# Turning the second attention's weights back unsplit, and placing them with sixteen transfers

## The chip, the cores and the metric

The kernel runs on one core of a Trainium2 chip. The metric is the device time of one execution in microseconds, lower is better. The engines are TensorE (PE in the profile, with its weight loads shown apart as PEld), VectorE (DVE), ScalarE (ACT), GpSimd (POOL) and SyncE (SP), which starts the transfers.

## The reference

Two attentions through 32 inducing points, and then a feed-forward layer with a squared ReLU, all in fp32:

```python
B, N, m, C = (4, 12480, 32, 128)          # attention
n_tokens, d_model, d_ff = (49920, 128, 2048)
...
def mab(q, kv):
    s = scale * (q @ kv.transpose(0, 2, 1))
    s = s - s.max(-1, keepdims=True)
    a = np.exp(s)
    a /= a.sum(-1, keepdims=True) + 1e-09
    return a @ kv
h = mab(I, x)          # I: the inducing points; 32 rows per batch
return mab(x, h)       # every token against those 32 rows
...
h = np.maximum(x @ w_in, 0.0)
return h * h @ w_out
```

## The kernel before

Tokens are worked on in 52 units of 960 (13 units for each of the 4 batches). A unit is two blocks of 480 tokens, and a block's 480 columns are four groups of 120. For every batch the first attention (class `First`) yields `h`, 32 rows, and `first_end` multiplies it by `w_in` once: `hw` holds `h @ w_in`, its rounded part and the rest stacked over partitions. So the second attention and the first layer of the feed-forward become one product: the attention weights of a block, 32 rows by 480 tokens, times `hw`. To get more than fp32r's precision out of fp32r products, the weights are split into a rounded part (`hi`) and the rest (`lo`), and stand stacked on 128 partitions in the tile `st` as hi, lo, hi, lo, one 480-wide slice for each of the two blocks.

How `st` comes about (class `Second`, `weigh`, from line 623): the scores of a unit (`na`, L617, written in `narrow` together with the First attention's scores of a later unit) are copied to SBUF (`ss`), turned by two fp32 transposes (`s2t`, L634) so that tokens lie on partitions, and go through maximum (L641), subtraction (L645), exponential (L648), sum (L652), a small addition on POOL (L656), reciprocal (L659) and the product `norm` (L662). The result `d` has 120 partitions and 256 columns. Then `high` (L692, a cast to fp32r into `sk`) and `low` (L696, `d` less its rounded part) split it on VectorE. `back` (L703) turns it again with four fp32r matmuls against the identity, which put block, hi or lo, and inducing point on 128 partitions (`ap`, in PSUM). `stacked` copies `ap` to `sw` in SBUF (480 columns; a helper, L247; ACT or DVE, whichever the planner finds free). `spread` (L718) starts four transfers on SP, each moving 64 partitions by 480 columns of `sw` to its place in `st`. The first unit of all (`first`) does this another way, with two tiles and without transfers.

The feed-forward part (`ffn_block`) reads `st`: 16 matmuls `h` (L821) for each block, then on ScalarE a ReLU (L833) and a square (L849), on VectorE a rounded part `hi` (L854) and the rest `lo` (L859), and on TensorE three products with the two parts of `w_out` that add up in `op` (L889). At the end of a block `op` is copied to `ot`, turned (`otp`, L909), copied to `osb` and stored.

Nothing is ordered by the loops. Each step is handed to a planner (`Plan`) as a task with an engine, an estimated duration, a due time, the tasks it needs and the PSUM banks or buffers that it takes and reads. `Plan.run` plays the tasks through: where several of an engine are ready it takes the one with the earliest due time, and the order that comes out is the fixed order in which each engine's instructions are issued. Due times repeat with a period of 32 us per unit. With t_u as the start of a unit in the plan, `narrow` for the next unit is due at t_u + 3 us, and the steps of `Second` follow at multiples of `step` = 4 us behind it: `norm` and the split at three steps, `back` at four (t_u + 19 us), `stacked` at five, `spread` at six. The next unit's first `h` is due 2 us before that unit begins (t_u + 30 us) and needs `spread`. The planner adds 2.5 us of latency to the end of a task on SP, and 0.25 us more ahead of an `h`.

Of the kernel before, what the change touches and what calls it, by code (L numbers as in the profile page):

```python
# [11 lines left out]
F32 = mybir.dt.float32  # L12
# [8 lines left out]
P = 128  # L21
# [23 lines left out]
class Plan:  # L45
# [8 lines left out]
    SWITCH = 95.0  # L54
    LATE = {"PE": 200.0, "other": 100.0}

    def __init__(self, room, begin):

        self.room, self.begin, self.tasks = room, begin, []
# [16 lines left out]
    def run(self):  # L76
# [37 lines left out]
        while len(done) < len(self.tasks):  # L114
            best = None
            for e in self.ENGINES:
                pick = None
                for t in open_[e]:
                    at = room_at(t) if t.takes else 0.0
                    if at is None:  # L120
                        continue
                    start = max(free[e], t.ready, at)
                    if e == "POOL" or (e == "DVE" and t.port):
                        start = max(start, port)
                    key = (0.0 if start <= free[e] + 40.0 else start, t.due, t.order)
                    if pick is None or key < pick[0]:
                        pick = (key, start, t)
# [27 lines left out]
def induced_attention_then_squared_relu_ffn(  # L155
# [28 lines left out]
    OB, SS, SS_NS = "DVE", "DVE", 317  # L184
    FUSED = set()
    G1_DUE, SQ_DUE, HI_DUE, LO_DUE, OP_DUE = -2000.0, 6000.0, 7000.0, 6000.0, 10500.0
# [13 lines left out]
    ps_o = ctx.enter_context(tc.tile_pool(name="ps_o", bufs=2, space=PSUM))  # L200
    ps_m = ctx.enter_context(tc.tile_pool(name="ps_m", bufs=2, space=PSUM))
    plan = Plan(dict(xn=3, early=6, xt=NU + 1, m=2, h=2, o=2, g=GB, hi=HB, lo=LB, st=2, sw=2), T_MAIN)
# [41 lines left out]
    ENG = {"ACT": nc.scalar.copy, "DVE": nc.vector.tensor_copy}  # L244
# [131 lines left out]
    class First:  # L376
        def __init__(self, b, u, due, early=False, begun=None):
# [15 lines left out]
            self.turned = []  # L393
            for k in range(2):
                self.turned.append(self.turn(k, due - lead + k * lead * 0.4, loaded))

        def turn(self, k, due, loaded):
# [18 lines left out]
            t = state["turn"] = add("PE", 440, turn, due, [loaded, state.get("turn"), self.begun] + self.turned,  # L416
# [12 lines left out]
        def weigh(self, scored, where, bank_, due):  # L429
# [25 lines left out]
            def turn_e():  # L455
                v["ep"] = bank(f"ep_{n}")
# [14 lines left out]
            t = add("PE", 300, turn_e, due + 2000, [self.powered], takes=[bank_e])  # L471
# [47 lines left out]
    def first_end(b, due, step):  # L519
# [80 lines left out]
        for k in range(F // 512):  # L600
            bw = Buffer("m" if b else "h")
            d = due + 2 * step + k * step + (WIDE_LATER if k and not b else 0)
            t = add("PE", 870, lambda k=k: wide(k), d, [s["joined"], w_ins[k]], takes=[bw])
# [4 lines left out]
    class Second:  # L608
# [13 lines left out]
        def weigh(self, scored, where, bank_, due, step):  # L622
# [8 lines left out]
            def turn():  # L631
                v["tp"] = tp = bank(f"s2t_{n}")
                for k in range(2):
# [55 lines left out]

            def high():  # L690
                v["sk"] = att.tile([TS, Q, 2, 2, M], F32R, tag="sk", name=f"sk_{n}")
                nc.vector.tensor_copy(v["sk"][:, :, :, 0, :], v["d"].rearrange("t (k q) m -> t q k m", q=Q))  # L692

            def low():
                sk = v["sk"]
                nc.vector.tensor_sub(  # L696
                    sk[:, :, :, 1, :], v["d"].rearrange("t (k q) m -> t q k m", q=Q), sk[:, :, :, 0, :]
                )

            def back():  # L700
                v["ap"] = ap = bank(f"ap_{n}")
                for q in range(Q):
                    nc.tensor.matmul(  # L703
                        ap[:, q * TS:(q + 1) * TS],
                        v["sk"][:, q].rearrange("t k a m -> t (k a m)"),
                        identr[:TS, :TS], start=(q == 0), stop=(q == Q - 1), skip_group_check=True,
                    )

            def stacked():

                v["sw"] = att.tile([P, BLK], F32R, tag="sw", name=f"sw_{n}")
                copy(ts, v["sw"], v["ap"][:, :BLK])

            def spread():
                st = att.tile([P, 2, BLK], F32R, tag="st", name=f"st_{n}")
                for k in range(2):
                    for j in range(2):
                        nc.sync.dma_start(  # L718
                            st[j * 64:(j + 1) * 64, k, :].bitcast(F32),
                            v["sw"][k * 64:(k + 1) * 64, :].bitcast(F32),  # L720
                        )
# [7 lines left out]
            t = add("PE", 150, turn, d + step, [te], takes=[bt])  # L729
            t = add("DVE", 340, top, d + step, [t], reads=[bt])  # L730
            td = add("DVE", 340, sub, d + step, [t], reads=[bt])
# [4 lines left out]
            tp = add("DVE", 340, norm, d + 3 * step, [t])  # L736
# [5 lines left out]
            else:  # L742
                th = add("DVE", 210, high, d + 3 * step, [tp], port=True)
                tl = add("DVE", 335, low, d + 3 * step, [th], port=True)
            if first:
                t1, last = [], None
                for k in range(2):
                    ba = Buffer("m")
                    t = add("PE", 460, lambda k=k: back1(k), d + (4 + k) * step, [ts_[k]], takes=[ba])
# [5 lines left out]
            t = add("PE", 460, back, d + 4 * step, [tl], takes=[ba])  # L755
            ts = add(ST, (455, 565), stacked, d + 5 * step, [t], takes=[bw], reads=[ba])
            self.ready = [add("SP", 1000, spread, d + 6 * step, [ts], takes=[self.bst], reads=[bw])] * 2

    def narrow(second, f, g, due, step, begun=None, early=False):
# [28 lines left out]
        if f:  # L788
            f.weigh(t, lambda: v["a"][:, 2 * TS:4 * TS], bank_a, due)
        if second:  # L790
            second.weigh(t, lambda: v["a"][:, :2 * TS], bank_a, due, step)
# [8 lines left out]
    def ffn_block(b, u, k, second, t0, g_open, by_pairs, fused):  # L800
# [7 lines left out]
        def quad(j, last):  # L808
# [4 lines left out]
            for i in range(2):  # L813
# [27 lines left out]
                if fused(j):  # L841
                    relus.append(add("DVE", 1090, relu, d + 1000, [t] + g_open + relus, late=100, **kw))
# [8 lines left out]
            def high(h):  # L851
                if h.start == 0:
                    v["hi"] = place(f"{n}_{j}", "hi")
                ENG["ACT" if fused(j) else "DVE"](v["hi"][:, h], v["g"][:, h])  # L854

            def low(h):
                if h.start == 0:
                    v["lo"] = place(f"{n}_{j}", "lo")
                nc.vector.tensor_sub(v["lo"][:, h], v["g"][:, h], v["hi"][:, h])  # L859

            from_hi, from_lo = [], []
            for x, h in enumerate(halves):
# [4 lines left out]
                if fused(j):  # L867
                    th = add("ACT", 1706, lambda h=h: high(h), due + 5700, need, late=0, **kw)
                else:
                    sq = add("ACT", 166 + 1540 * part_of, lambda h=h: square(h), due + SQ_DUE + off, need, reads=[bg], late=0)  # L870
                    th = add("DVE", 70 + 1000 * part_of, lambda h=h: high(h), due + HI_DUE + off, [sq] + from_hi, port=True,
                             late=0 if x or len(halves) > 1 else LATE_HI, **kw)
                tl = add("DVE", 70 + 2000 * part_of, lambda h=h: low(h), due + LO_DUE + off + 900 * (len(halves) > 1), [th] + from_lo, port=True, late=100.0 * fused(j),
                         takes=[blo] if x == 0 else [], reads=[bg, bhi] + ([blo] if x else []))
# [7 lines left out]
            for x, (m, i) in enumerate(order):  # L882
# [12 lines left out]
                last = add("PE", 438, products, due + OP_DUE - ahead + 600 * x, [from_[i if len(halves) > 1 else 0], last, w_outs[j]],  # L895
# [118 lines left out]
```

## Time and profile before

| | us |
|---|---|
| three runs | 1733.75, 1734.13, 1734.22 (median 1734.13) |
| the profiled execution, its own time | 1733.3 |
| its span, first to last instruction | 1731.5 |
| TensorE busy | 1709.3 |
| VectorE busy | 1649.1 |
| ScalarE busy | 1625.9 |

The profile shows one execution. A busy time is the union of an engine's instructions. Rows of groups give a source line, the engine, the operation, `out<-in` tiles, sizes and a count; behind the first bar stand the busy microseconds and the mean nanoseconds of one instruction; behind the second the idle time of the engine just before them and what ended it. Rows in order of time begin with the start and the duration in microseconds. Rows by window begin with the window and its length, and give the busy time of each engine (or of the chosen tile's instructions) with counts, the granted clock, the share of the DMA engines that is busy and GB/s. Matmuls are pipelined: one of 480 columns is shown with some 0.38 us, but the next starts about 0.2 us after it. The granted TensorE clock over the span was 0.998 of full speed.

### The profile page before, as it was taken

The page shows a single profiled execution, that of the slowest core. Times are in us where ns is not written, and L with a number is a line of the kernel's source. Part 1 is how long each engine was busy: PE and PEld are TensorE (multiplying, and loading weights), DVE is VectorE, ACT ScalarE, POOL GpSimd, SP SyncE. Part 2 cuts the span into 40 slices and gives each one's busy share as a digit, 9 for nine tenths or more (in the row PEclk, how much of TensorE's full clock was granted, in tenths as well). Part 3 has the DMA queues.
Part 4 walks back from the last instruction along what each step waited for, and adds up shares of the span by engine and source line. Part 5 has one row for each costly group of instructions (what it writes and reads, how often), then busy time and mean ns, then how long its engine had stood idle before and what let it go on. Part 6 is the DMA issues. An engine that isn't in the chain of part 4 may idle for free.

```text
span 1731.5 us, 24820 instructions
## 1 busy us (share of the span) xinstructions
PE 1709.3 (99%) x9629; PEld 1426.2 (82%) x9629; DVE 1649.1 (95%) x1744; ACT 1625.9 (94%) x1725; POOL 24.0 (1%) x57
## 2 busy tenths in 40 slices
PE   7899999999999999999999999999999999999998
PEld 5588888888888888888878888888888888888887
DVE  5999999999999999999999999999999999999998
ACT  6799999999999999999999999999999999999997
POOL 0000000000000000000000000000000000000000
PEclk9999999999999999999999999999999999999999
DMA  9211211211121111212211111111110111111110
GB/s 243 50 48 48 51 41 49 52 45 48 28 53 46 46 47 46 58 37 50 52 35 47 46 46 47 50 43 47 41 28 23 45 25 35 35 35 35 27 43 23
DMA packets 34068, 82.00 MB, mean 47 GB/s; under 512 B 4983, under 2 KB 21079, under 8 KB 33951
## 3 DMA queue, kind: packets, MB, share of 16 engines
q1 hardware_dynamic: 33951, 80.42, 18.7%
q8 instruction: 76, 1.25, 0.3%
q14 instruction: 41, 0.34, 0.1%
HBM read 29.77 MB, written 25.56 MB: 32 GB/s over the span
## 4 chain that ended last, share of the span: by engine, by line
PE 96%; DVE 1%; DMA 1%; ACT 1%; issue 0%; SPq 0%; DVEq 0%; ACTq 0%
PE op L889 63%; PE h L821 21%; PE otp L909 3%; PE xtp L409 2%; PE na L617 2%; DMA xn<-in_x_dram 1%; PE ap L703 1%; PE nb L479 1%; PE na L424 1%; PE wp L575 1%; PE s2t L634 1%; PE ep L458 1%; DVE lo L859 0%; PE sp L424 0%; ACT e L450 0%
## 5 line engine op out<-in xcount | busy, mean ns | idle before, releaser
L859 DVE TENSOR_TENSOR lo<-g,hi 128x1920 fp32r<-128x1920 f32 (+1 forms) x419 | 896.6, 2140 | 19.5 <-DVE hi L854 0.9
L833 ACT ACTIVATE g<-h 128x960 f32<-128x960 f32 x832 | 794.3, 979 | 26.3 <-PE h L821 23.6
L849 ACT ACTIVATE g<-g 128x1920 f32<-128x1920 f32 (+1 forms) x419 | 757.3, 1808 | 3.9
L821 PE MATMUL h<-st,hw 128*128 128x480 f32 x1664 | 512.2, 387 | 2.1 <-ACT g L833 1.2
L854 DVE CAST hi<-g 128x1920 fp32r<-128x1920 f32 (+1 forms) x419 | 480.2, 1146 | 32.2 <-ACT g L849 20.5
L889 PE MATMUL op<-hi,wo_lo 128*128 128x480 f32 x1664 | 500.5, 383 | 0.0
L889 PE MATMUL op<-hi,wo_hi 128*128 128x480 f32 x1664 | 467.9, 389 | 0.1
L889 PE MATMUL op<-lo,wo_hi 128*128 128x480 f32 x1664 | 435.4, 382 | 0.0
L889 PEld LDWEIGHTS op<-lo,wo_hi 128*128 128x128 f32 x1664 | 309.8, 188 | 50.4 <-DVE lo L859 0.2
L889 PEld LDWEIGHTS op<-hi,wo_lo 128*128 128x128 f32 x1664 | 309.4, 188 | 48.7 <-issue 1.0
L889 PEld LDWEIGHTS op<-hi,wo_hi 128*128 128x128 f32 x1664 | 301.7, 188 | 55.2 <-issue 12.6
L821 PEld LDWEIGHTS h<-st,hw 128*128 128x128 f32 x1664 | 302.1, 188 | 47.7 <-ACT g L833 2.7
L247 DVE COPY osb<-otp 120x512 f32<-120x512 f32 x104 | 71.0, 683 | 2.6 <-PE otp L909 2.5
L409 PE MATMUL xtp<-ident,xn 120*128 120x120 f32 x416 | 61.5, 275 | 4.5 <-DMA xn<-in_x_dram 4.2
L409 PEld LDWEIGHTS xtp<-ident,xn 120*128 120x128 f32 x416 | 50.7, 145 | 17.4 <-issue 4.0
L247 ACT COPY ot<-op 128x480 f32<-128x480 f32 x80 | 45.4, 567 | 20.4 <-PE op L889 20.3
L909 PE MATMUL otp<-ident,ot 128*120 128x128 f32 x416 | 62.5, 273 | 1.0 <-ACT ot L247 0.6
L909 PEld LDWEIGHTS otp<-ident,ot 128*120 128x120 f32 x416 | 50.6, 137 | 15.1 <-DVE hw L584 1.8
L247 ACT COPY xt<-xtp 128x480 f32<-128x480 f32 x66 | 37.6, 574 | 13.4 <-PE xtp L409 13.4
L656 POOL TENSOR_SCALAR z<-z 120x8 f32<-120x8 f32 x51 | 23.3, 456 | 1649.0 <-DVE z L652 1649.0
L703 PEld LDWEIGHTS ap<-identr,sk 120*128 120x128 f32 x204 | 30.0, 190 | 3.7
L479 PE MATMUL nb<-xn,et 120*32 120x128 f32 x752 | 32.8, 277 | 0.0
(113 smaller groups left out, 690.4 us busy)
## 6 DMA issues: line engine op xcount, KB each, us to landing
xn<-in_x_dram SPq DMA_DIRECT2D x52, 480.0 KB, 4.3
st<-sw SPq DMA_DIRECT2D x204, 120.0 KB, 2.3
out_dram<-osb SPq DMA_DIRECT2D x51, 480.0 KB, 3.3
hi_i<-in_moe_w_in_dram SPq DMA_DIRECT2D x2, 512.0 KB, 13.3
lo_i<-in_moe_w_in_dram SPq DMA_DIRECT2D x2, 512.0 KB, 15.4
hi_o<-in_moe_w_out_dram SPq DMA_DIRECT2D x2, 512.0 KB, 11.5
lo_o<-in_moe_w_out_dram SPq DMA_DIRECT2D x2, 512.0 KB, 11.2
out_dram<-osb SPq DMA_DIRECT2D x2, 240.0 KB, 2.6
```

Source lines behind the costliest of these rows:

```text
L247: ENG[task.by](dst, src)
L409: nc.tensor.transpose(v["tp"][:, t * TS:(t + 1) * TS], self.xn[:, 4 * k + t, :], ident[:TS, :TS])
L479: nc.tensor.matmul(where[q * M:(q + 1) * M, :], self.et[:, k, q * M:(q + 1) * M], self.xn[:, 2 * q + k, :], start=(k == 0), stop=(k == 1),)
L617: nc.tensor.matmul(where[q * M:(q + 1) * M, :], self.s["hT"][:, :M], self.s["xt"][self.u][:, q * 2 * TS:(q + 1) * 2 * TS], start=True, sto ...
L703: nc.tensor.matmul(ap[:, q * TS:(q + 1) * TS], v["sk"][:, q].rearrange("t k a m -> t (k a m)"), identr[:TS, :TS], start=(q == 0), stop=(q ...
L821: nc.tensor.matmul(c["hp"][:, l, :BLK], s["hw"][:, f * P:(f + 1) * P], s["st", u][:, k, :], start=True, stop=True,)
L833: nc.scalar.activation(g, h, AF.Relu)
L849: nc.scalar.activation(v["g"][:, h], v["g"][:, h], AF.Square)
L854: ENG["ACT" if fused(j) else "DVE"](v["hi"][:, h], v["g"][:, h])
L859: nc.vector.tensor_sub(v["lo"][:, h], v["g"][:, h], v["hi"][:, h])
L889: nc.tensor.matmul(w["op"][:, :BLK], wo[:, 4 * j + l, :], v[name][:, l, :], start=(j == x == 0 and l == 0), stop=(j == NQ - 1 and x == 5 a ...
L909: nc.tensor.transpose(tp[:TS, q * P:(q + 1) * P], w["ot"][:, q * TS:(q + 1) * TS], ident)
```

## The change

For every unit but the first of all, `norm`'s result is turned back as it is, by two fp32 transposes, one per block. On 128 partitions lie now column group and inducing point, in the columns the two blocks of 120 tokens. The split follows in PSUM's layout: `high` copies 240 columns to fp32r (ACT or DVE), `low` on DVE subtracts that from what PSUM holds. Both parts go to `sw`. Since a column group's 32 rows must now go to other columns, and hi and lo are each wanted twice, `spread` starts sixteen transfers, each moving 32 partitions by two runs of 120 columns (30 KB).

The planner's table of costs is altered with it: `spread` is charged 1600 ns instead of 1000, PE tasks carry a mode, changes of mode and some durations have new values. The diff brings several new switches as well (turning pairs together, work on POOL, another division of PSUM banks, a preference for the same mode), all at the value at which the old way is kept: `PAIR = XTP_PAIR = False`, `STICK = 0.0`, `FUSED`, `POOL_HI` and `POOL_LO` empty, `MB = 2`.

```diff
-            def high():
-                v["sk"] = att.tile([TS, Q, 2, 2, M], F32R, tag="sk", name=f"sk_{n}")
-                nc.vector.tensor_copy(v["sk"][:, :, :, 0, :], v["d"].rearrange("t (k q) m -> t q k m", q=Q))
-
-            def low():
-                sk = v["sk"]
-                nc.vector.tensor_sub(
-                    sk[:, :, :, 1, :], v["d"].rearrange("t (k q) m -> t q k m", q=Q), sk[:, :, :, 0, :]
-                )
-
             def back():
                 v["ap"] = ap = bank(f"ap_{n}")
-                for q in range(Q):
-                    nc.tensor.matmul(
-                        ap[:, q * TS:(q + 1) * TS],
-                        v["sk"][:, q].rearrange("t k a m -> t (k a m)"),
-                        identr[:TS, :TS], start=(q == 0), stop=(q == Q - 1), skip_group_check=True,
+                for k in range(2):
+                    nc.tensor.transpose(
+                        ap[:, k * TS:(k + 1) * TS],
+                        v["d"][:, k * Q:(k + 1) * Q].rearrange("t q m -> t (q m)"), ident[:TS, :TS],
                     )
 
-            def stacked():
-
-                v["sw"] = att.tile([P, BLK], F32R, tag="sw", name=f"sw_{n}")
-                copy(ts, v["sw"], v["ap"][:, :BLK])
+            def high():
+                v["sw"] = att.tile([P, 2, 2 * TS], F32R, tag="sw", name=f"sw_{n}")
+                copy(th, v["sw"][:, 0], v["ap"][:, :2 * TS])
+
+            def low():
+                nc.vector.tensor_sub(v["sw"][:, 1], v["ap"][:, :2 * TS], v["sw"][:, 0])
 
             def spread():
                 st = att.tile([P, 2, BLK], F32R, tag="st", name=f"st_{n}")
-                for k in range(2):
-                    for j in range(2):
+                for q in range(Q):
+                    for a in range(4):
                         nc.sync.dma_start(
-                            st[j * 64:(j + 1) * 64, k, :].bitcast(F32),
-                            v["sw"][k * 64:(k + 1) * 64, :].bitcast(F32),
+                            st[a * M:(a + 1) * M, :, q * TS:(q + 1) * TS].bitcast(F32),
+                            v["sw"][q * M:(q + 1) * M, a % 2, :].rearrange("p (k t) -> p k t", k=2).bitcast(F32),
                         )
...
-            tp = add("DVE", 340, norm, d + 3 * step, [t])
+            tp = add("DVE", 340, norm, d + 3 * step, [t], port=True)
...
-                th = add("DVE", 210, high, d + 3 * step, [tp], port=True)
-                tl = add("DVE", 335, low, d + 3 * step, [th], port=True)
...
-            t = add("PE", 460, back, d + 4 * step, [tl], takes=[ba])
-            ts = add(ST, (455, 565), stacked, d + 5 * step, [t], takes=[bw], reads=[ba])
-            self.ready = [add("SP", 1000, spread, d + 6 * step, [ts], takes=[self.bst], reads=[bw])] * 2
+            t = add("PE", 219, back, d + 4 * step, [tp], takes=[ba], mode="t")
+            th = add(ST, (255, 317), high, d + 5 * step, [t], takes=[bw], reads=[ba])
+            tl = add("DVE", 317, low, d + 5 * step, [th], reads=[ba, bw])
+            self.ready = [add("SP", 1600, spread, d + 6 * step, [tl], takes=[self.bst], reads=[bw])] * 2
...
-    SWITCH = 95.0
+    SWITCH = {"t": 0.0, "r": 0.0, "n": 100.0, None: 0.0}
...
+        return cls.SWITCH[old] if new is None else 92.0 if new == "n" != old else 0.0
...
-                if t.mode != mode:
-                    start += self.SWITCH
+                start += self.switch(mode, t.mode)
...
-            t = add("PE", 300, turn_e, due + 2000, [self.powered], takes=[bank_e])
+                t = add("PE", 219, turn_e, due + 2000, [self.powered], takes=[bank_e], mode="t")
...
-            t = add("PE", 150, turn, d + step, [te], takes=[bt])
+                t = add("PE", 219, turn, d + step, [te], takes=[bt], mode="t")
...
-        t = add("PE", 510 * bool(second) + 520 * bool(f) + 450 * bool(g), go, due, needs, mode="n",
+        t = add("PE", 445 * bool(second) + 410 * bool(f) + 470 * bool(g), go, due, needs, mode="n",
```

More of the change, by code (lines that the diff above doesn't have):

```diff
@@ L185, in induced_attention_then_squared_relu_ffn @@
     FUSED = set()
+    POOL_HI = set()
+    POOL_LO = set()
+    FUSED_DUE = 3000.0
+    STICK = 0.0
+    PAIR, PAIR_DUE, XTP_PAIR = False, 3000.0, False
+    MB = 2
     G1_DUE, SQ_DUE, HI_DUE, LO_DUE, OP_DUE = -2000.0, 6000.0, 7000.0, 6000.0, 10500.0
@@ L243, in induced_attention_then_squared_relu_ffn @@
     add = plan.add
-    ENG = {"ACT": nc.scalar.copy, "DVE": nc.vector.tensor_copy}
+    ENG = {
+        "ACT": nc.scalar.copy, "DVE": nc.vector.tensor_copy,
+        "POOL": lambda dst, src: nc.gpsimd.tensor_scalar(dst, src, 1.0, 0.0, ALU.mult, ALU.add),
+    }
     def copy(task, dst, src):
@@ L393, in __init__, with turn_both, turn, turned @@
             self.turned = []
+            if XTP_PAIR and not early:
+                self.turn_both(due - lead, loaded)
+                return
             for k in range(2):
                 self.turned.append(self.turn(k, due - lead + k * lead * 0.4, loaded))
+        def turn_both(self, due, loaded):
+            banks = [Buffer("m"), Buffer("m")]
+            tp = {}
+            def turn():
+                self.xt = self.s["xt"][self.u] = xt_pool.tile([C, UNIT], F32, tag="xt", name=f"xt_{self.n}")
+                for k in range(2):
+                    tp[k] = bank(f"xtp_{self.n}_{k}")
+                    for t in range(4):
+                        nc.tensor.transpose(tp[k][:, t * TS:(t + 1) * TS], self.xn[:, 4 * k + t, :], ident[:TS, :TS])
+            t = state["turn"] = add("PE", 750, turn, due, [loaded, state.get("turn"), self.begun], mode="t",
+                                    takes=banks + [self.bt], reads=[self.bx])
+            for k in range(2):
+                def turned(k=k):
+                    copy(self.turned[k], self.xt[:, k * BLK:(k + 1) * BLK], tp[k][:, :BLK])
+                self.turned.append(add(XT[k], (440, 567), turned, due + XT_DUE, [t], reads=[banks[k], self.bt]))
         def turn(self, k, due, loaded):
@@ L620, in score, with weigh @@
                 )
-        def weigh(self, scored, where, bank_, due, step):
+        def weigh(self, scored, where, bank_, due, step, pair=None):
             v = {}
@@ L728, in weigh, with turn_both, with_e @@
             te = add(SS, SS_NS, evict, d, [scored], reads=[bank_])
-            t = add("PE", 150, turn, d + step, [te], takes=[bt])
-            t = add("DVE", 340, top, d + step, [t], reads=[bt])
-            td = add("DVE", 340, sub, d + step, [t], reads=[bt])
+            if pair is None:
+                t = add("PE", 219, turn, d + step, [te], takes=[bt], mode="t")
+            else:
+                def turn_both():
+                    turn()
+                    pair["e"]()
+                def with_e(turn_e, powered):
+                    pair["e"] = turn_e
+                    pair["task"] = add("PE", 438, turn_both, d + PAIR_DUE, [te, powered], takes=[bt], mode="t")
+                    return pair["task"]
+                pair.update(bank=bt, turn=with_e)
+                t = pair["first"]()
+            t = add("DVE", 340, top, d + max(step, PAIR_DUE if pair else 0), [t], reads=[bt])
+            td = add("DVE", 340, sub, d + max(step, PAIR_DUE if pair else 0), [t], reads=[bt])
             tp = add("ACT", 307, power, d + 2 * step, [td])
@@ L894, in quad @@
                 begin = j == x == 0
-                last = add("PE", 438, products, due + OP_DUE - ahead + 600 * x, [from_[i if len(halves) > 1 else 0], last, w_outs[j]],
+                last = add("PE", 438, products, due + OP_DUE - ahead + 600 * x, [from_[min(i, len(from_) - 1)], last, w_outs[j]],
                            takes=[bo] if begin else [], reads=[buf] + ([] if begin else [bo]))
```

91 lines of the change are left out of this document (58 added, 33 removed).

## The prediction

> **What bounds the kernel now.** I read the page first: its busy shares, then its chain of work that ended last.
>
> ```profile
> span 1731.5 us, 24820 instructions
> PE 1709.3 (99%) x9629; PEld 1426.2 (82%) x9629; DVE 1649.1 (95%) x1744; ACT 1625.9 (94%) x1725; POOL 24.0 (1%) x57
> PE 96%; DVE 1%; DMA 1%; ACT 1%; issue 0%; SPq 0%; DVEq 0%; ACTq 0%
> ```
>
> TensorE (PE) is busy in all but 22 us of the span, and the chain of waits runs through it for 96%. VectorE (DVE) and ScalarE (ACT) are nearly as full, but nothing waits for them for long. So the end is set by the amount of work on PE, and by any moment at which PE stands still. A microsecond taken from DVE or ACT is worth nothing by itself; one PE idle per unit is worth 51 us.
>
> Next I asked the view by tile for `st`, the stacked weights, and counted the `h` matmuls, their readers, with the view by windows.
>
> ```profile
> L821 PE MATMUL h<-st,hw x1664: 372/381/778, 62.8 to 1716.0; 128*128 128x480 f32 x185
> L718 SPq DMA_DIRECT2D st<-sw x204: 461/590/1428, 86.1 to 1683.9; - x102
> DMA to landing us min/median/max: 2.1/2.3/4.1
> ```
> ```profile
> 0.00:610.44 610.44, 168.22 (x545) 0.99 0.24 61
> 610.44:642.60 32.16, 9.71 (x32) 1.00 0.19 47
> ```
>
> 52 units share 1664 `h` matmuls, 32 each, so matmul 545, at 610.44, is the first of unit 17 (counted from 0): the first that reads the weights which unit 17's transfers bring. Unit 18's first comes 32.2 us later. Now the whole making of those weights, from the view of instructions in order of time (single instructions picked out by narrow windows):
>
> ```profile
> 598.83 0.42 DVE L662 TENSOR_TENSOR d<-d,z 120x256 f32<-120x256 f32 x1
> 600.23 0.29 DVE L692 CAST sk<-d 120x256 fp32r<-120x256 f32 x1
> 602.50 0.42 DVE L696 TENSOR_TENSOR sk<-d,sk 120x256 fp32r<-120x256 f32 x1
> 603.29 0.56 PE L703 MATMUL ap<-identr,sk 120*128 120x120 f32 x4
> 604.56 0.53 ACT L247 CAST sw<-ap 128x480 fp32r<-128x480 f32 x1
> 605.12 0.47 SPq L718 DMA_DIRECT2D st<-sw  x1
> 605.64 0.59 SPq L718 DMA_DIRECT2D st<-sw  x1
> 606.28 0.59 SPq L718 DMA_DIRECT2D st<-sw  x1
> 606.91 0.59 SPq L718 DMA_DIRECT2D st<-sw  x1
> 610.22 0.38 PE L889 MATMUL op<-lo,wo_hi 128*128 128x480 f32 x1
> 610.44 0.38 PE L821 MATMUL h<-st,hw 128*128 128x480 f32 x1
> ```
>
> The normalised weights are ready at 599.25, the turn back starts at 603.29, the copy ends at 605.09, and the four transfers start 0.52, 0.64 and 0.63 us after one another. The last lands about 2.3 us after its issue, at 609.2, and `h` reads at 610.44 behind PE work without a gap: 1.2 us to spare. The transfers are hidden now, but by little.
>
> **PE's own work.** Four `back` matmuls become two fp32 transposes, which are what `s2t` does now. From the view of groups, 300 to 1600 us:
>
> ```profile
> L703 PE MATMUL ap<-identr,sk 120*128 120x120 f32 x164 | 22.8, 261 | 0.0
> L634 PE MATMUL s2t<-ident,ss 128*120 128x128 f32 x80 | 15.2, 272 | 0.0
> ```
>
> Four `ap` take 22.8/41 = 0.56 us, two transposes 15.2/40 = 0.38, so a unit saves 0.18 and 51 units 9 us; counted by halves (two of four matmuls, 0.28 a unit) it is 14. I take 10.
>
> **DVE and ACT.** The split moves behind the turn: the cast and subtraction on DVE (0.29 + 0.42) and a 480-wide copy (0.53 on ACT) become a 240-wide copy and a subtraction that reads PSUM. Their nearest rows:
>
> ```profile
> L645 DVE TENSOR_TENSOR d<-s2t,mx 120x256 f32<-120x256 f32 x40 | 16.8, 420 | 0.4
> L247 ACT COPY et<-ep 120x256 f32<-120x256 f32 x30 | 11.0, 367 | 0.3 <-PE ep L458 0.2
> ```
>
> DVE saves about 0.3 us a unit and ACT 0.16. PE's work covers both engines, so I count nothing; without that cover it would be some 15 us of DVE. The split's bank stays taken for one DVE instruction longer; PE has other work then, nothing counted.
>
> **The planner.** Every new switch (PAIR, XTP_PAIR, STICK, FUSED, the POOL sets, MB = 2) stands at its neutral value. New durations, modes and the port on `norm` can only reorder. The most a better order can give is the 22 us that PE idles; what a worse one costs no row shows. Zero, with 10 us either way.
>
> **The transfers: when `back` runs and when `h` wants its weights.** The planner lets the earliest due go first when PE has a choice: `back` is due 19 us after a unit's start, the next unit's first `h` 30 us after it. Neither due changes. Today `back` comes late because it waits for cast and subtraction; after the change it needs only `norm`, so it can run 0.37 after it (the step from 602.92 to 603.29): 599.6, which is 10.8 us ahead of 610.44 and about its due. In unit 18 `norm` is further ahead, and the due takes over:
>
> ```profile
> 628.34 0.42 DVE L662 TENSOR_TENSOR d<-d,z 120x256 f32<-120x256 f32 x1
> 633.46 0.56 PE L703 MATMUL ap<-identr,sk 120*128 120x120 f32 x4
> 642.63 0.38 PE L821 MATMUL h<-st,hw 128*128 128x480 f32 x1
> ```
>
> 13.9 us from `norm` to `h`, but 11 between the two dues. I take 10.8 for all 51 units. The planner charges the sixteen transfers 1.6 us plus 2.5 to land, so it sees its weights ready in good time and has no reason to move `h` back.
>
> The way from `back` to the landing: two transposes 0.38; the wait for the copying engine 0.71 (603.85 to 604.56); copy 0.37; the wait for DVE, between nothing and one `lo` (2.15) and 1.98 for `sk` at 600.52, taken as 1.5; subtraction 0.42; to SP 0.03. That makes 3.4.
>
> Then sixteen transfers of 32 rows with two runs each, 64 pieces like the 64 rows of today. No row has that shape. The nearest is today's `st<-sw`, 0.52 for the first and 0.635 for each later one; from below, loads issued one right after another at the start, and one alone:
>
> ```profile
> 2.07 0.41 SPq L390 DMA_DIRECT2D xn<-in_x_dram  x1
> 2.53 0.40 SPq L335 DMA_DIRECT2D hi_i<-in_moe_w_in_dram  x1
> 2.97 0.51 SPq L390 DMA_DIRECT2D xn<-in_x_dram  x1
> 616.89 0.33 SPq L390 DMA_DIRECT2D xn<-in_x_dram  x1
> ```
>
> They stand 0.45 apart. I take `st`'s own price, the same rows between the same memories: the sixteenth starts 0.52 + 14 x 0.635 = 9.4 us after the first and lands at 9.4 + 2.3 = 11.7. At 0.45 it would be 15 x 0.45 + 2.1 = 8.9. Each transfer carries both blocks' columns, so the first `h` needs all sixteen. They land 3.4 + 11.7 = 15.1 us after `back`, and PE arrives after 10.8: it stands still 4.3 us a unit, 51 x 4.3 = 219 us (1.5 us, 77 in all, at 0.45). Behind the waiting `h` on PE stand the older block's `op` products and the next `xtp`, ready but not reachable, and ACT and DVE run dry behind PE. On SP the sixteen end some 10 us after about 603, before the load at 616.89; the next store is later still. Both keep their time.
>
> **What standing still does to the clock.** The windows with their granted clock (the number after the busy shares), and PE's gaps before them:
>
> ```profile
> 48.00:50.00 2.00, 0.38 (x3) 0.32 (x3) 2.00 (x8) 1.06 (x2) 0.00 (x0) 0.59 0.84 209
> 50.00:52.00 2.00, 1.62 (x11) 0.56 (x11) 1.65 (x5) 0.00 (x0) 0.00 (x0) 0.50 0.17 61
> 52.00:54.00 2.00, 2.00 (x7) 0.85 (x4) 1.17 (x3) 0.00 (x0) 0.00 (x0) 0.50 0.00 0
> 54.00:56.00 2.00, 2.00 (x9) 1.14 (x7) 1.43 (x4) 0.79 (x2) 0.00 (x0) 0.71 0.00 0
> 60.00:64.00 4.00, 2.26 (x18) 1.46 (x16) 3.91 (x10) 1.88 (x6) 0.00 (x0) 1.00 0.00 0
> ```
> ```profile
> 45.73 0.43 PE L458 MATMUL ep<-ident,e 128*120 128x128 f32 x2 [1.20 <-ACT e L450]
> 49.89 0.77 PE L562 MATMUL htp<-join,hacc 128*128 128x128 f32 x2 [1.62 <-DVE join L558]
> ```
>
> With gaps no longer than 1.62 us the clock was halved for about 1.6 + 2 + 2 + 1.2 = 6.8 us; at 60 to 64 us, with PE idle for 1.7 of 4, it held. A gap of 4.3 us is longer than any of these. If half of such a stretch, 3.4 us, falls on matmuls, a stall costs another 1.7; I take it for four stalls in five, 1.4 a unit, 70 us. The ends are 0 and 3.4 a unit. By the Trainium skill ("TensorE: Matmul & The Clock Gate", Part 1) the clock halves only after a whole idle window of about 3.4 us, in a row of windows that runs freely; a 4.3 us gap covers one about one time in four, and by that rule I estimate 20 us here and a sum near 1960. The trace above differs, as it halved with shorter gaps.
>
> **The sum.** The profiled execution took 1733.3 us (span 1731.5 and 1.8 around it), 0.05% under the 1734.13 median. 1733.3 - 10 + 219 + 70 = 2012 us, slower.
>
> **The rivals.** *All hidden.* If the transfers start no more than 0.35 us apart, the last lands 3.4 + 15 x 0.35 + 2.1 = 10.8 after `back`, just in time; only PE's saving is left: 1723. For it speaks the lone load's 0.33; against it, the median `st` transfer keeps SP for 0.59 by itself. The Trainium skill ("DMA: Bandwidth & Descriptors", Issuing engines are not separate DMA queues) would have it so: the time a sequencer needs to start a transfer is usually small beside the transfer. Here it is 0.635 against 2.3, and sixteen make 10; the trace disagrees. Chance 0.12.
>
> *Half hidden.* The transfers stand 0.45 apart, like loads: 1.5 us a unit, too short to halve the clock: 1733 - 10 + 77 = 1800. For it speaks the halved row count, against it the equal number of pieces. Chance 0.14.
>
> *Stall without the clock.* As forecast, but the clock holds, as at 60 to 64 us: 1733 - 10 + 219 = 1942. Chance 0.2.
>
> *Stall with more.* The whole 6.8 us of each halved stretch fall on matmuls: 1723 + 51 x (4.3 + 3.4) = 2116, or over 2130 if a transfer costs more than 0.635 by its two runs a row. Over 2130: 0.04.
>
> **How the numbers follow.** The forecast has 0.5. From 1780, under the half-hidden case, to 2130, over the full price of the clock, the range holds all but the hidden case and the top, and a little of the half-hidden one. A measurement of this kernel can tell about 0.2%, 3.5 us, from no change. Faster 0.12 (hidden), same 0.02 (hidden but for the last 0.2 us a unit), slower 0.86.
>
> **What would show it.** In the changed profile: 816 `st<-sw` transfers in groups of sixteen, about 10 us long; a gap of about 4 us before the first `h` of each unit, put down to a DMA; PE's share near 85%; granted clock under 0.95; `back` starting within 1 us of `norm` or about 11 us of PE work before `h`. Starts 0.35 us apart or less would make it wrong, and so would `h` standing 15 us of PE work behind `back`.

## The result, and the profile after

The changed kernel takes 2075.74 us (median of 4 runs, 2075.06 to 2077.81) against 1734.18 (median of 4 runs beside it) before: ratio 1.197, 95% interval 1.195 to 1.198. Its profiled execution took 2075.06, 341.8 more than the 1733.3 of the one before.

The page of the changed kernel, span, busy shares and the chain of work that ended last:

```profile
span 2073.2 us, 25260 instructions
PE 1806.5 (87%) x9527; PEld 1489.5 (72%) x9527; DVE 1635.7 (79%) x1707; ACT 1627.7 (79%) x1711; POOL 31.6 (2%) x57
PE 50%; SPq 21%; DVE 15%; issue 6%; DMA 5%; ACT 3%; POOL 0%; DVEq 0%; ACTq 0%
```

PE is busy for 87% instead of 99%, and the chain, 96% on PE before, now runs for a fifth through SP's own instructions. Two things stand in the first two lines: PE idles 2073.2 - 1806.5 = 267 us where it idled 22, and its busy time has grown although two of its matmuls per unit were taken away. The views by tile and of waits say for what PE idles:

```profile
L753 SPq DMA_DIRECT2D st<-sw x816: 585/594/1921, 81.3 to 2026.1; - x164
DMA to landing us min/median/max: 1.8/1.9/3.7
```
```profile
PE h L878 <- DMA st<-sw: 217.6, 45, 6.6
```

The idle time before `h`, in the kernel before and in the changed one:

```profile
L821 PE MATMUL h<-st,hw 128*128 128x480 f32 x1664 | 512.2, 387 | 2.1 <-ACT g L833 1.2
L878 PE MATMUL h<-st,hw 128*128 128x480 f32 x1664 | 543.5, 410 | 244.2 <-DMA st<-sw 217.6
```

Each of the 816 transfers keeps SP for 0.59 us, like the 204 before, though it has half the rows and a quarter of the bytes (before and after it moves 64 contiguous pieces). Unit 17 in order of time, from the turn back to the unit's first `h` (line 878; matmul 545 of its kind, as before; the row with sixteen transfers gives their whole stretch):

```profile
709.14 0.37 PE L737 MATMUL ap<-ident,d 120*128 120x120 f32 x2
709.55 0.41 DVE L264 CAST sw<-ap 128x240 fp32r<-128x240 f32 x1
709.87 2.15 DVE L916 TENSOR_TENSOR lo<-g,hi 128x1920 fp32r<-128x1920 f32 x1
709.99 13.11 SPq L753 DMA_DIRECT2D st<-sw  x16
711.94 1.16 DVE L911 CAST hi<-g 128x1920 fp32r<-128x1920 f32 x1
713.01 0.40 DVE L747 TENSOR_TENSOR sw<-ap,sw 128x240 fp32r<-128x240 f32 x1
724.55 0.67 PE L878 MATMUL h<-st,hw 128*128 128x480 f32 x2 [4.13 <-DMA st<-sw]
```

The first transfer, of a rounded part, starts before the subtraction has run; the second carries a rest and waits for it, and with it all behind it on SP. From 713.44 fifteen follow, the last starts at 722.50 and lands 1.9 later, at 724.4. PE has been idle for 4.13 us. These rows were picked out with narrow windows:

```profile
713.44 0.59 SPq L753 DMA_DIRECT2D st<-sw  x1
722.50 0.59 SPq L753 DMA_DIRECT2D st<-sw  x1
```

The windows around that gap, with the granted clock behind the busy times:

```profile
720.00:724.00 4.00, 0.42 (x5) 0.19 (x2) 3.15 (x3) 0.58 (x2) 0.00 (x0) 1.00 0.22 51
724.00:726.00 2.00, 1.45 (x5) 1.26 (x6) 0.00 (x0) 0.75 (x1) 0.00 (x0) 0.83 0.00 0
726.00:728.00 2.00, 2.00 (x6) 1.65 (x5) 0.00 (x0) 1.92 (x2) 0.00 (x0) 0.50 0.00 0
728.00:730.00 2.00, 2.00 (x9) 1.71 (x8) 0.94 (x1) 0.97 (x1) 0.00 (x0) 0.81 0.00 0
```

Just when PE has work again, its clock is halved for 0.7 + 2 + 0.8 = 3.4 us. The mean granted clock over the span is 0.933, which makes (1 - 0.933) x 2073.2 / 0.5 = 278 us at half speed.

### The profile page after: what moved, and what is told of

The parts are those of the page before. It is cut to its first block, busy times and chain, and to the rows that moved or that the text cites. A ratio compares the mean times of both kernels' runs of the same rounds, so it can differ in the third digit from the quotient of the medians.

```text
span 2073.2 us, 25260 instructions
## 1 busy us (share of the span) xinstructions
PE 1806.5 (87%) x9527; PEld 1489.5 (72%) x9527; DVE 1635.7 (79%) x1707; ACT 1627.7 (79%) x1711; POOL 31.6 (2%) x57
## 4 chain that ended last, share of the span: by engine, by line
PE 50%; SPq 21%; DVE 15%; issue 6%; DMA 5%; ACT 3%; POOL 0%; DVEq 0%; ACTq 0%
PE op L955 31%; SPq L753 21%; PE h L878 12%; DVE lo L916 6%; DVE hi L911 5%; DMA st<-sw 5%; PE na L659 1%; PE nb L521 1%; ACT g L906 1%; ACT g L890 1%; DVE sw L264 1%; PE otp L975 1%; DVE sw L747 1%; PE na L463 1%; PE xtp L448 1%
## 5 line engine op out<-in xcount | busy, mean ns | idle before, releaser
L890 ACT ACTIVATE g<-h 128x960 f32<-128x960 f32 x832 | 786.3, 976 | 358.1 <-PE h L878 355.3
L878 PE MATMUL h<-st,hw 128*128 128x480 f32 x1664 | 543.5, 410 | 244.2 <-DMA st<-sw 217.6
L878 PEld LDWEIGHTS h<-st,hw 128*128 128x128 f32 x1664 | 320.2, 201 | 307.2 <-issue 258.5
L955 PE MATMUL op<-hi,wo_lo 128*128 128x480 f32 x1664 | 528.3, 401 | 0.0
L955 PE MATMUL op<-hi,wo_hi 128*128 128x480 f32 x1664 | 506.0, 414 | 0.0
L955 PEld LDWEIGHTS op<-hi,wo_lo 128*128 128x128 f32 x1664 | 330.2, 201 | 54.8 <-issue 1.4
L955 PEld LDWEIGHTS op<-hi,wo_hi 128*128 128x128 f32 x1664 | 323.7, 203 | 58.6 <-issue 12.0
L955 PEld LDWEIGHTS op<-lo,wo_hi 128*128 128x128 f32 x1664 | 319.9, 193 | 54.9 <-DVE lo L916 0.3
L264 ACT COPY xt<-xtp 128x480 f32<-128x480 f32 x97 | 53.4, 554 | 45.9 <-PE xtp L448 45.9
L659 PE MATMUL na<-xt,hT 128*32 128x240 f32 x416 | 32.7, 386 | 0.4 <-DVE hT L264 0.4
## 6 DMA issues: line engine op xcount, KB each, us to landing
hi_i<-in_moe_w_in_dram SPq DMA_DIRECT2D x2, 512.0 KB, 13.1
```

The lines of the kernel that those rows point to most:

```text
L264: ENG[task.by](dst, src)
L659: nc.tensor.matmul(where[q * M:(q + 1) * M, :], self.s["hT"][:, :M], self.s["xt"][self.u][:, q * 2 * TS:(q + 1) * 2 * TS], start=True, sto ...
L878: nc.tensor.matmul(c["hp"][:, l, :BLK], s["hw"][:, f * P:(f + 1) * P], s["st", u][:, k, :], start=True, stop=True,)
L890: nc.scalar.activation(g, h, AF.Relu)
L955: nc.tensor.matmul(w["op"][:, :BLK], wo[:, 4 * j + l, :], v[name][:, l, :], start=(j == x == 0 and l == 0), stop=(j == NQ - 1 and x == 5 a ...
```

## The experiments

The theory is that of the prediction: sixteen transfers start one after another on SP, PE reaches the next unit's first `h` before the last has landed, stands still, and then works at a halved clock. The rivals: the split behind the turn comes too late whatever the number of transfers; small pieces are slow to land; the planner's new order costs by itself. `e1` to `e12` count the runs.

### Four transfers instead of sixteen (e1)

```diff
-                for q in range(Q):
-                    for a in range(4):
+                for k in range(2):
+                    for j in range(2):
                         nc.sync.dma_start(
-                            st[a * M:(a + 1) * M, :, q * TS:(q + 1) * TS].bitcast(F32),
-                            v["sw"][q * M:(q + 1) * M, a % 2, :].rearrange("p (k t) -> p k t", k=2).bitcast(F32),
+                            st[j * 64:(j + 1) * 64, k, :].bitcast(F32),
+                            v["sw"][k * 64:(k + 1) * 64].rearrange("p a t -> p (a t)").bitcast(F32),
```

> The changed kernel, but its weights leave in four transfers of 64 partitions by 480 columns instead of sixteen; the same bytes land in st, in other columns than they should (the pieces are not put in their right places). Theory, the count of transfers on SP: the last lands some 4.2 us after the subtraction, 4.3 + 4.2 = 8.5 us after the turn back, where PE arrives after 10.7; no gap before a unit's first h, clock at 0.998, 1715 to 1730 us, about 10 below the kernel before. Rival, the split behind the turn comes too late: the chain from the turn to the subtraction is unchanged, so gaps of some us per unit remain and the time stays over 1800. Rival, the planner's new order costs: no gap before h, but a time above 1745.

1724.8 us, ratio 0.994 (0.993 to 0.995). The page:

```profile
span 1723.7 us, 24412 instructions
PE 1701.4 (99%) x9527; PEld 1416.5 (82%) x9527; DVE 1633.2 (95%) x1707; ACT 1616.4 (94%) x1711; POOL 31.6 (2%) x57
```

The readers of `st`:

```profile
L878 PE MATMUL h<-st,hw 128*128 128x480 f32 x1664 | 509.8, 388 | 0.4 <-ACT g L890 0.4
```

With everything of the change but the count of transfers (and the pieces' right places in `st`), the loss is gone, PE no longer waits before `h`, and its saving is there: 10 us against the kernel before in the medians, 7.8 between the profiled spans. The split behind the turn and the new order cost nothing that can be seen. This run is also the measure for the rest: against it the changed kernel's PE idles 266.7 - 22.3 = 244 us more and is busy for 1806.5 - 1701.4 = 105 us more with the same 9527 matmuls. 244 + 105 is the whole distance between the two spans, 349.5.

### Sixteen transfers in the kernel before (e2)

```diff
-                for k in range(2):
-                    for j in range(2):
-                        nc.sync.dma_start(
-                            st[j * 64:(j + 1) * 64, k, :].bitcast(F32),
-                            v["sw"][k * 64:(k + 1) * 64, :].bitcast(F32),
-                        )
+                for q in range(Q):
+                    for j in range(2):
+                        for k in range(2):
+                            nc.sync.dma_start(
+                                st[j * 64:(j + 1) * 64, k, q * TS:(q + 1) * TS].bitcast(F32),
+                                v["sw"][k * 64:(k + 1) * 64, q * TS:(q + 1) * TS].bitcast(F32),
+                            )
```

> The kernel before, its four transfers cut into sixteen (64 partitions by 120 columns each, the same bytes in the right places). Theory, the count alone: 0.52 + 13 x 0.635 us until the fifteenth starts and 1.9 to land make 10.7 us from the copy, where the first h came 6.0 us after it on average: PE stands 4.7 us per unit, 240 us, and the halved clock adds about 110: 2030 to 2110 us. Rival, the split in PSUM or the planner's order causes the loss: the kernel keeps within 1% of 1734. Rival, half the rows make a transfer dear: starts here, with 64 rows each, are clearly less than 0.6 us apart and the time is under 1900.

2091.8 us, ratio 1.206 (1.204 to 1.208). Nothing but the number of transfers differs from the kernel before. The readers of `st`, and the transfers:

```profile
L822 PE MATMUL h<-st,hw 128*128 128x480 f32 x1664 | 550.1, 412 | 245.1 <-DMA st<-sw 233.0 <-issue 10.7 <-ACT st L247 0.6
L719 SPq DMA_DIRECT2D st<-sw x816: 461/595/1714, 87.2 to 2041.3; - x164
```

Before `h` PE idles 245.1 us, 4.8 a unit, as in the changed kernel. With 64 rows a transfer keeps SP as long (0.595) as with 32, so the rows set no price here; each is 64 pieces in both. Count alone is enough, and e1 and e2 together clear the other parts of the change.

### The gap filled with idle work (e3)

```diff
                         c["hp"] = ps_h.tile([P, 2, 512], F32, tag="h", name=f"h_{n}_{2 * j + i}")
+                        if k == j == i == 0 and (b, u) != units[0]:
+                            for _ in range(20):
+                                nc.tensor.matmul(
+                                    c["hp"][:, 0, :BLK], s["hw"][:, :P], s["hw"][:, :BLK], start=True, stop=True,
+                                )
```

> The changed kernel, with 20 matmuls of 480 columns put ahead of each unit's first h, into the same PSUM bank that it then overwrites; they need nothing that is late and fill about 4.1 us of the gap of 4.2 to 6.6. Theory, the halved clock costs over 100 us of the 341: the gap shrinks to under 1.5 us, the clock goes back to above 0.98, and the time falls to 1950 to 1980 although PE has 51 x 4.1 us more to do. Rival, the halved clock costs nothing of its own (other engines set the pace then): the time stays at 2075 within 10. A third way, that the gap is not a wait for transfers at all: the matmuls add their 210 us and the time goes to 2280.

1989.1 us (ratio 1.146, 1.145 to 1.148), 87 less than the changed kernel and just above the range expected. Page and readers of `st`:

```profile
span 1986.7 us, 27300 instructions
PE 1933.5 (97%) x10547; PEld 1606.6 (81%) x10547; DVE 1635.0 (82%) x1707; ACT 1621.7 (82%) x1711; POOL 31.6 (2%) x57
L883 PE MATMUL h<-st,hw 128*128 128x480 f32 x1664 | 512.1, 389 | 30.5 <-DMA st<-sw 23.2 <-issue 5.9 <-ACT g L895 1.3
```

The kernel does 1020 useless matmuls more and is faster. The mean clock is 0.995; the real `h` take 389 ns in the mean, as without stalls, and 30.5 us of gaps are left. The halved clock is thus a cost of its own, and the gap is a real wait: filling it added nothing. It came out above the range in part because the 20 matmuls made PE busy for (1933.5 - 1701.4) / 51 = 4.6 us a unit and not 4.1, longer than half of the gaps of the changed kernel; the rest stays open.

### Another order of the same transfers (e4)

```diff
-                for q in range(Q):
-                    for a in range(4):
+                for a in (0, 2, 1, 3):
+                    for q in range(Q):
```

> The changed kernel with its sixteen transfers in another order: the eight that carry the rounded parts first, then the eight that carry the rest. Now the second transfer waits for the subtraction, 3.4 us after the first starts. Theory, SP's time counts from when its transfers can run without a wait: the last starts 9.4 us after the first instead of 12.4, the gap falls from 4.8 to about 1.8 us, the clock recovers in part: 1820 to 1925 us. Rival, the landing of many small pieces is the limit and not their start: the last lands as late as now and the time stays above 2030.

1890.5 us, ratio 1.089 (1.088 to 1.091). The readers, and one group of sixteen on SP:

```profile
L878 PE MATMUL h<-st,hw 128*128 128x480 f32 x1664 | 523.5, 397 | 114.8 <-DMA st<-sw 89.4 <-issue 12.2 <-ACT xt L264 12.0
654.05 10.23 SPq L753 DMA_DIRECT2D st<-sw  x16
```

The same transfers end in 10.2 us instead of 13.1, since eight of them run while the subtraction is still waiting for VectorE. The gaps fall to 114.8 us, 2.3 a unit. One line of order in a queue is worth 185 us. Landing was not the limit.

### The planner told the true cost (e5)

```diff
-            self.ready = [add("SP", 1600, spread, d + 6 * step, [tl], takes=[self.bst], reads=[bw])] * 2
+            self.ready = [add("SP", 10500, spread, d + 6 * step, [tl], takes=[self.bst], reads=[bw])] * 2
```

> The changed kernel, with the planner told what sixteen transfers cost on SP (10500 ns instead of 1600), nothing else. Theory, a loop from one unit's first h to the next: first h, narrow, some 13 us to norm, then 15.2 us to the landing, over 32 us in all; moving h back in the order brings no other work into the gap. The planner's own plan grows by 200 us, and the time stays far above the kernel before: 1880 to 2060 us, the gap spread over other places. Rival, the 1600 in the table is the fault and an honest cost lets PE's other work cover the wait: 1720 to 1760 us.

1909.6 us, ratio 1.100 (1.098 to 1.102). No gap is left before a unit's first `h`, as the planner now puts other work there, but the time is not given back. Its readers and the longest wait of PE's weight loads:

```profile
L878 PE MATMUL h<-st,hw 128*128 128x480 f32 x1664 | 514.5, 397 | 46.5 <-ACT g L890 46.5
PEld h L878 <- ACT g L890: 80.4, 106, 2.3
```

PE now waits for ScalarE's ReLU instead, for 46.5 of its 113.5 us of idle time. It is also busy for 1795.8 - 1701.4 = 94 us more than in e1, of which its clock (0.987) accounts for no more than (1 - 0.987) x 1909.3 = 25; the rest stays open. So the 1600 was wrong, but an honest number alone does not hide the transfers. The loop that the expectation names fits the time; that it is the loop and nothing else was not shown.

### The chain moved ahead (e6, e8)

```diff
-    PERIOD, START, T_MAIN, NARROW, STEP = 32000.0, 2600.0, 46000.0, 3000.0, 4000.0
+    PERIOD, START, T_MAIN, NARROW, STEP = 32000.0, 2600.0, 46000.0, 1000.0, 3000.0
...
-            self.ready = [add("SP", 1600, spread, d + 6 * step, [tl], takes=[self.bst], reads=[bw])] * 2
+            self.ready = [add("SP", 7000, spread, d + 6 * step, [tl], takes=[self.bst], reads=[bw])] * 2
```

e8 is this edit alone; e6 has e4's order too.

> The rounded parts' transfers first, as before, and the whole chain moved ahead: narrow due 1 us after a unit's start instead of 3, steps of 3 us instead of 4, SP charged 7000. In the plan the turn back now stands 12.9 to 15.1 us ahead of the next unit's first h instead of about 11, and the last landing is due 12.4 after the turn. Theory: gaps under 0.5 us, clock above 0.99, PE's saving is all that is left: 1720 to 1740 us. Rival, earlier dues take places from PE's other work, which then waits for VectorE and ScalarE: no gap before h, but 1745 to 1800 us.

> The changed kernel with the chain moved ahead (narrow at 1 us, steps of 3 us, SP charged 7000) and the transfers in the change's own order. The last landing comes 15.2 us after the turn, and the plan puts 12.9 to 15.1 between turn and h. Theory: a gap of 0.2 to 1 us in most units and 2 in some, clock near 0.99: 1735 to 1790 us; the lead alone gives back more than the order alone (1890). Rival, what the order alone gave came from the wait of SP's queue and not from the lead: still above 1850.

e6: 1734.4 us, ratio 0.9995 (0.9986 to 1.0003). e8: 1747.4, ratio 1.007 (1.006 to 1.009). The readers of `st` in e6:

```profile
L878 PE MATMUL h<-st,hw 128*128 128x480 f32 x1664 | 509.5, 387 | 6.0 <-ACT g L890 4.5 <-DMA st<-sw 1.2 <-issue 0.3
```

Sixteen transfers can be hidden: their waits shrink to 1.2 us. But 10 us against e1 are lost elsewhere, some 6 of them as PE's idle time (1731.8 - 1703.1 = 28.7 against 22.3), and PE's saving is spent. The lead alone is worth far more than the order alone (1747 against 1890).

### Half of the transfers on POOL (e7, e11)

```diff
-            self.ready = [add("SP", 1600, spread, d + 6 * step, [tl], takes=[self.bst], reads=[bw])] * 2
+            ts = add("SP", 1600, spread, d + 6 * step, [th], takes=[self.bst], reads=[bw])
+            tq = add("POOL", 1600, lambda: spread(nc.gpsimd, (1, 3)), d + 6 * step, [tl, ts], reads=[bw, self.bst])
+            self.ready = [tq] * 2
```

`spread` takes a queue and the two places that it fills. e11 adds narrow at 2.5 us, steps of 3.5 us and a charge of 100 on POOL.

> The changed kernel; the eight transfers of the rounded parts start on SP as soon as those are copied, the eight of the rest start on POOL after the subtraction. No transfer of POOL's is in any trace here, so its price is open. Theory, what is serial is the issuing engine: SP's eight end 5.1 us after the copy; if POOL starts its eight as fast as SP, the last lands 4.3 + 5.1 + 1.9 = 11.3 us after the turn against 10.7 available: 1740 to 1800 us; at 1 us each on POOL 14.2 us and 1930 to 1990. Rival, the transfers are serial in the DMA engines that both share: the last lands about 14 to 15 us after the turn whatever the queue, with POOL's instructions short, and the time stays above 1950.

> Eight transfers on SP and eight on POOL, with narrow due at 2.5 us and steps of 3.5 us; the plan puts the turn 12.9 us ahead of the first h in most units. The last landing came 10.9 us after the turn with this split. Theory: no gap in most units, 1725 to 1745 us. Rival, POOL's transfers hold up its small addition in the chain to norm and VectorE beside it: no gap before h, but 1760 to 1815.

e7: 1817.4 us, ratio 1.048 (1.046 to 1.049); e11: 1745.3, ratio 1.006 (1.004 to 1.007). In e7:

```profile
L755 SPq DMA_DIRECT2D st<-sw x408: 585/594/1730, 84.1 to 1766.1; - x136
L755 POOL DMA_DIRECT2D st<-sw x408: 533/536/1538, 87.8 to 1767.7; - x136
```

POOL starts a transfer in 0.53 us, SP in 0.59 beside it: what is serial is the engine that starts them, not what moves the bytes. It shows best in unit 14 of e11, where both start at nearly the same time and each takes for its eight about what SP takes alone, 5.1 us:

```profile
514.62 5.07 SPq L755 DMA_DIRECT2D st<-sw  x8
515.36 5.21 POOL L755 DMA_DIRECT2D st<-sw  x8 [5.56 <-DVE sw L747]
```

e7 came out above the first of its two ranges and below the second, though POOL is as fast as the first assumed and the last landing came 10.9 us after the turn in the mean. In the 46 units with a gap, the first `h` began 0.85 us behind the last landing (0.28 in the changed kernel); why is not shown. Against e1, PE idles 88.3 - 22.3 = 66 us more and is busy for 1727.9 - 1701.4 = 26.5 us more, at a mean clock of 0.986. e11 stands just above the range expected; its gaps before a unit's first `h` add up to 15.5 us, in six units, the longest 3.6, and not to none.

### By way of DRAM in six transfers (e9, e10, e12)

```diff
-                for q in range(Q):
-                    for a in range(4):
-                        nc.sync.dma_start(
-                            st[a * M:(a + 1) * M, :, q * TS:(q + 1) * TS].bitcast(F32),
-                            v["sw"][q * M:(q + 1) * M, a % 2, :].rearrange("p (k t) -> p k t", k=2).bitcast(F32),
-                        )
+                for a in range(2):
+                    away = dram.tile([P, 2 * TS], F32, tag=f"away{a}", name=f"away_{n}_{a}")
+                    nc.sync.dma_start(away, v["sw"][:, a, :].bitcast(F32))
+                    for j in range(2):
+                        rows = slice((2 * j + a) * M, (2 * j + a + 1) * M)
+                        nc.sync.dma_start(
+                            st[rows].rearrange("m k (q t) -> m k q t", q=Q).bitcast(F32),
+                            away.rearrange("(q m) (k t) -> m k q t", q=Q, k=2),
+                        )
```

`dram` is a new pool of buffers in DRAM. e10 adds steps of 3.5 us and a charge of 2500 on SP; e12 narrow at 2.5 us, steps of 3.5 us and a charge of 5000.

> The changed kernel, its weights sent to their places by way of DRAM: one transfer writes the rounded part away as it stands (128 partitions by 240 columns), two read it back into its two places with columns in order, and the same for the rest: six transfers in all, every one in the right place. The writes must land before the reads start. Nothing in the planner changes. No trace here shows such a pair; a store lands about 3.3 us after its issue at 480 KB and 2.6 at 240 KB. Theory, what counts is the time from the subtraction to the last landing: about 2.2 for the write, 0.6 for the start of the second read, 2.5 to land, 5.3 us, 9.6 after the turn against 10.7: no gap in most units, 1722 to 1735 us, against 1725 for four transfers in wrong places. Rival, reading runs of 480 bytes back from DRAM is slow (over 4 us): gaps of 1 to 2 us, 1780 to 1850.

> As by way of DRAM, with steps of 3.5 us instead of 4 and SP charged 2500, by which the plan puts the turn 12 us instead of 11 ahead of the next unit's first h. Theory: one microsecond more of room; if the variant before it has gaps, they go: 1720 to 1730 us, below the kernel before by 0.3 to 0.7%. Rival, the earlier chain costs PE's other work, as the longer lead may have done: above 1732.

> By way of DRAM, narrow due at 2.5 us, steps of 3.5 us, SP charged 5000. What is left of gaps in the two variants before stands at the first units of a batch, where norm comes late: 1.5 to 3 us each. The higher charge makes the planner put at least 10.0 us between turn and h there too, 12.9 in most units, and its plan is 1.6 us longer than the changed kernel's. Theory: no gap over 0.5 us before an h, 1724 to 1732 us, 0.2 to 0.6% below the kernel before. Rival, reordering costs PE more than the gaps did, as with the longest lead (1734): 1734 to 1745.

e9: 1754.3 us, ratio 1.011 (1.009 to 1.012). e10: 1742.8, ratio 1.004 (1.003 to 1.005). e12: 1726.8, ratio 0.996 (0.994 to 0.997). The first two missed: their gaps, 18.7 and 12.0 us before `h` in sum, stand in few units, the longest at the first units of a batch. e12 gives those units room. It is within its range, though its longest gap is 1.35 us and not under 0.5, and it is below both kernels, by 8 us or 0.4% below the one before:

```profile
span 1724.0 us, 24674 instructions
PE 1697.6 (98%) x9527; PEld 1411.8 (82%) x9527; DVE 1615.5 (94%) x1633; ACT 1638.1 (95%) x1785; POOL 35.7 (2%) x57
L882 PE MATMUL h<-st,hw 128*128 128x480 f32 x1664 | 514.7, 390 | 4.0 <-DMA st<-away 2.4 <-ACT g L894 1.3 <-issue 0.3
```

## Why the prediction was right

**PE's saving.** Taken as 10 us, measured by e1 as 10 in the medians and 7.8 between the spans.

**Where `back` runs and when `h` comes.** 10.8 us of PE work were put between them; in unit 17 it is 724.55 - 709.14 - 4.13 = 11.3, over the 51 units 10.7 in the mean (the start of the first `h` less that of the turn less the gap). Neither due moved, as argued.

**From the turn to SP.** 3.4 us were put together; it took 713.41 - 709.14 = 4.3. The missing 0.9 is the wait for DVE: two long instructions (`lo`, 2.15, and `hi`, 1.16) stand ahead of the subtraction, 3.05 us, where 1.5 was taken. The copy went to DVE and not to ACT and waited for nothing, which gave 0.7 back.

**The transfers.** 11.7 us were put from the end of the subtraction to the last landing; it took 10.9 (713.41 to 724.4), because the first ran ahead of the subtraction and each landed in 1.9 instead of 2.3. The price of a start was right: (722.50 - 713.44) / 14 = 0.647 against 0.635. That the errors of these two terms cancelled is luck: 15.1 us forecast from turn to landing, 15.2 measured. That one blocked transfer holds up the fourteen behind it was not seen; e4 shows what it is worth.

**The stall.** 4.3 us a unit and 219 in all were forecast, 244.2 us (4.8 a unit) stand before `h`. Of the 0.5 us more, 0.28 is the mean time from the last landing to the start of the first `h`, which the sum left out. Unit 17 has 4.1, and the gaps are longest after a change of batch and in the last quarter, where PE has less than 10.8 us of work between.

**The clock.** This term was mis-sized: 70 us forecast, 105 measured as PE's growth in busy time, and 87 given back when e3 filled the gaps. Two of its steps failed. One is "four stalls in five": by the trace's record of the clock every one of the 51 stalls was followed by a halved stretch, which at the 1.7 us a stall of the prediction makes 87. The other is the 3.4 us of matmuls in a stretch: the stretches last 3.4, 6.8 or 10.2 us, 270/51 = 5.3 in the mean, and PE works in 214/51 = 4.2 of it, so a stall costs 2.1 us more and not 1.7.

**The sum.** -10 + 244 + 105 = 339, against 341.8 measured between the two profiled executions (with the 7.8 of the spans the sum closes) and 279 forecast. Of the rivals, "all hidden" and "half hidden" needed starts 0.35 or 0.45 us apart; no `st` transfer on SP took under 0.585. "Stall without the clock" falls with e3. By the Trainium skill ("DMA: Bandwidth & Descriptors", Issuing engines are not separate DMA queues) the time to start a transfer is usually small beside the transfer. That does not carry over to a queue of sixteen: 0.59 us each against 1.9 to land, and e7 and e11 show that the start is what limits.

## What to carry to other kernels

Count the transfers of a step, not their bytes: the last of n that one engine starts begins n - 1 times the price of a start after the first and lands later still, and a planner or a sum that charges the step as one thing misses it. Before moving work behind a wait, compare that whole chain with the work that the bottleneck engine has until it needs the result; a microsecond missing there was paid here nearly one and a half times, once as idle time and again at the halved clock. Where transfers depend on different producers, put those that can run ahead of those that must wait.

## What the runs showed of the hardware that was not expected

A single stall of some 2 us is enough for the clock of TensorE to halve. In e4 the gaps before the first `h` of a unit vary from 0.95 to 5.82 us. By the trace's record of the clock, none of the 24 gaps under 2.0 us was followed by a halved stretch, 23 of the 27 longer ones were, and so were all 51 in the changed kernel (3.4 to 6.6 us). A gap of 1.22 us in e4, at 665.72, left the clock alone:

```profile
662.00:666.00 4.00, 2.78 (x17) 2.27 (x15) 4.00 (x4) 2.65 (x4) 0.00 (x0) 1.00 0.18 38
666.00:668.00 2.00, 2.00 (x11) 1.72 (x10) 1.22 (x1) 1.58 (x2) 0.00 (x0) 1.00 0.00 0
```

What sorts the four exceptions is where a gap falls. In the trace's record of the clock all changes lie whole multiples of 3.41 us apart. Cut at these points, the changed kernel, e2 and e4 have, behind their first 100 us and ahead of their last 8, 1366 such windows at full clock in which PE idled for at most 1.89 us, and none of them was followed by a halved one; in 123 it idled for 1.91 us or more, and all were. In e4 the gap of 2.70 us before unit 40's first `h` lies in two windows, 1.84 and 0.86, and the clock stays; unit 38's 2.04 lies in one, and it halves:

```profile
1463.73:1467.15 3.42, 1.58 (x8) 1.01 (x6) 3.32 (x4) 2.01 (x2) 0.00 (x0) 1.00 0.21 51
1467.15:1470.56 3.41, 2.55 (x12) 2.25 (x13) 1.73 (x1) 1.85 (x2) 0.00 (x0) 1.00 0.01 3
1388.64:1392.05 3.41, 1.37 (x6) 0.65 (x4) 2.03 (x3) 1.28 (x2) 0.00 (x0) 1.00 0.15 36
1392.05:1395.47 3.42, 3.42 (x23) 2.66 (x23) 2.19 (x2) 2.66 (x2) 0.00 (x0) 0.50 0.02 5
```

Idle time is not the whole rule: in the first 100 us and in e5, windows with less of it (from 1.2 and 1.47 us) were followed by halved ones too. By the Trainium skill ("TensorE: Matmul & The Clock Gate", Part 1) it takes a whole idle window of about 3.4 us. The 3.41 us of this record agree with that length; the 1.9 us of idle time that were enough do not, and the measurement decides.

What a transfer costs the engine that starts it does not grow with its rows or its bytes: 0.59 us from SBUF to SBUF with 32 or 64 rows (e2), 0.60 for e9's reads from DRAM into 32 rows of `st` (median of 204), 0.33 for the load of 480 KB at 616.89 in the kernel before, and 0.34 for e9's write of 128 rows to DRAM. What does set it was not tested. The write:

```profile
548.24 0.34 SPq L754 DMA_DIRECT2D away<-sw  x1
```
